# First layer of a channel MLP as seven products of weight and token quarters

## The chip, the core and the metric

The kernel runs on one core of a Trainium2 chip. TensorE (PE) multiplies 128 x 128 weights by up to 512 columns and sums in PSUM; VectorE (DVE), ScalarE (ACT) and GpSimd (POOL) work on tiles in SBUF and PSUM (POOL here on SBUF alone); SyncE (SP) issues the DMAs. PEld is the load of PE's weights beside the running matmul. The metric is the device time in microseconds, lower is better. Before the change the median of 3 runs is 773.5 us (773.27 to 777.58).

## The reference

Three blocks follow each other, all in float32, for 4 batches of 576 tokens and 512 channels (2304 tokens in all):

```python
scores = where(block_i >= block_j, q @ k.T / sqrt(64), -1e9)   # 8 heads of 64, blocks of 64 tokens
x = softmax(scores) @ v
xk, xr = mu_k * x + (1 - mu_k) * x_prev, mu_r * x + (1 - mu_r) * x_prev
k = relu(xk @ w_k)                                             # 512 -> 1024
x = sigmoid(xr @ w_r) * (k * k @ w_v)                          # 1024 -> 512
u = x + (relu(x.T @ w_tok1) @ w_tok2).T                        # 576 -> 256 -> 576, over tokens
out = u + relu(u @ w_ch1) @ w_ch2                              # 512 -> 1536 -> 512
```

## The kernel before

**Precision.** Outside the attention every float32 operand is split into a high part (a cast to PE's fp32r) and a low part (what the cast lost), and a product is three: high x high, high x low, low x high, summed in PSUM. `copy` (L487) makes a high part, `less` (L490) a low one; either may stand on several engines.

**Stages.** The attention comes first. `channel_mix` does the second block, its products in the l banks of PSUM (L961 for the high parts, L966 for the low ones; wx and wy are the two places in SBUF that hold its weights). It stores its result r to DRAM (xd, L1073). `front` does the token MLP of one batch: it loads x from xd (L1094), PE transposes it (L1099), `hidden` (L1123) and `back_in` (L1144) are its two layers, `sum_u` leaves u in the place of x. `back` does the channel MLP in five chunks of the 2304 token columns: chunk 0 has 256, chunks 1 to 4 have 512 each.

**A chunk of the back stage.** ACT and DVE split u (uh, L1245; ul, L1248). Each of twelve groups of 128 hidden channels is 12 matmuls over all columns of the chunk into one of six PSUM banks b (L974); relu takes it to g (L1262, or ACT). The second layer is seven products of quarters already: weights, g and the output are each cut in 2 x 2 quarters, seven sums or differences of g's quarters are multiplied by seven sums or differences of the weight's, and the outputs are added up. `term` (L1204) makes the sums of g, `operand` their high and low parts (op, four buffers), `product` (L1222) is 36 matmuls of 256 columns into one of two PSUM tiles x, with weights that `fetch` (L1213) loads from DRAM wd into one of three buffers rg, 1.5 MB each. `add` (L1295) adds an output to u, the result, which L1300 stores. Chunk 0 does both layers as two plain block products.

**Weights.** The weight of the first layer, c1, lies where channel mix had its own weights (wx), and each half of that is free when channel mix needs it no more (the gates wrfree, wkfree). The weight comes in pieces wst (L516) whose upper 16 bits DVE or ACT bring together (tw, L487), which DVE joins, and of which the high and low parts are written (wx). `load_c2` does the second layer's in twelve column groups: it loads and joins (L1394, L1404), writes the parts into wo, makes the differences of quarters in ws (L1437), writes their parts into wo too and stores wo to wd (L1449).

**Order.** Each step is recorded with its engine or choice of engines; two long tables, RANK (a rank for each step) and ON (its engine), set the order of every engine's queue, and a planner only hands out the buffers. An engine works its queue in order: a step that waits holds up all behind it. Three gates separate stages: sw1 (attention done), sw2 (channel mix done: its PSUM and SBUF become x2, x3, g, the tiles x), sw3 (token MLP and weights done: op1 to op3 and rg).

Of the kernel before, what the change touches and what calls it, by code (L numbers as in the profile page):

```python
# [466 lines left out]
class Kern:  # L467
# [615 lines left out]


    def front(self, b, pool, gate):

        nc, step = self.nc, self.step
        c = {}
        tx = self.tu[b] = Buf()
        self.plan.group = f"f{b}"  # L1090
# [4 lines left out]

# [274 lines left out]
    def load_c2(self, stage):  # L1370
# [5 lines left out]
        for q in range(2 * NH):  # L1376
# [9 lines left out]
            for x in range(2):  # L1386
# [328 lines left out]
```

## Time and profile before

| | us |
|---|---|
| median of 3 runs | 773.5 |
| profiled execution | 776.2 |
| its span | 774.3 |
| PE busy | 754.7 |
| DVE busy | 584.2 |
| ACT busy | 415.7 |
| POOL busy | 276.6 |

The granted TensorE clock is at its upper level in all 40 slices. The span is one execution on the chip by the profiler, and the execution's own time stands above it by what lies around the span. Busy time counts instructions on the engine alone, not its waits. The mean over the span mixes the attention, the token MLP and the back stage, so the slices, the windows and the chain of waits belong to the reading. In a row, "out<-in" are the program's names, and "idle before <-" is the time that the engine stood before such an instruction and what released it. A duration of PE in the groups counts the pipelined instruction whole; the pace of a run of matmuls is its length over their number.

### The profile page before, as it was taken

The page shows a single profiled execution, that of the slowest core. Times are in us where ns is not written, and L with a number is a line of the kernel's source. Part 1 is how long each engine was busy: PE and PEld are TensorE (multiplying, and loading weights), DVE is VectorE, ACT ScalarE, POOL GpSimd, SP SyncE. Part 2 cuts the span into 40 slices and gives each one's busy share as a digit, 9 for nine tenths or more (in the row PEclk, how much of TensorE's full clock was granted, in tenths as well). Part 3 has the DMA queues.
Part 4 walks back from the last instruction along what each step waited for, and adds up shares of the span by engine and source line. Part 5 has one row for each costly group of instructions (what it writes and reads, how often), then busy time and mean ns, then how long its engine had stood idle before and what let it go on. Part 6 is the DMA issues. An engine that isn't in the chain of part 4 may idle for free.

```text
span 774.3 us, 17660 instructions
## 1 busy us (share of the span) xinstructions
PE 754.7 (97%) x6745; PEld 686.5 (89%) x6745; DVE 584.2 (75%) x1336; ACT 415.7 (54%) x1128; POOL 276.6 (36%) x276
## 2 busy tenths in 40 slices
PE   7899999989999999999999999999999999999998
PEld 5677889988999899999999998889989998999997
DVE  8899999988989999895998798744144663974392
ACT  6899988789877787873645455321023112211220
POOL 5441342134433131242434126122343342862351
PEclk9999999999999999999999999999999999999999
DMA  8779894997847867649289857452544644765685
GB/s 273 262 186 215 161 161 114 172 164 134 166 117 127 169 130 153 98 90 291 73 278 292 298 165 244 164 222 93 189 177 163 258 172 175 267 215 215 212 297 202
DMA packets 149700, 146.26 MB, mean 189 GB/s; under 512 B 105456, under 2 KB 127600, under 8 KB 145008
## 3 DMA queue, kind: packets, MB, share of 16 engines
q1 hardware_dynamic: 149616, 145.13, 67.7%
q8 instruction: 53, 0.87, 0.5%
q14 instruction: 31, 0.25, 0.1%
HBM read 98.44 MB, written 22.02 MB: 156 GB/s over the span
## 4 chain that ended last, share of the span: by engine, by line
PE 83%; DMA 8%; DVE 5%; ACT 2%; issue 1%; POOL 0%; SPq 0%; DVEq 0%; ACTq 0%
PE l L961 20%; PE b L974 19%; PE x L1222 16%; PE l L966 9%; DMA pt<-pin 6%; PE s L700 5%; PE o L868 4%; PE b L1123 4%; PE b L1144 3%; PE b L1099 1%; DMA v<-in_v 1%; DVE op L490 1%; DVE nm L737 1%; DMA stage<-in_w_k 1%; ACT pin L494 1%
## 5 line engine op out<-in xcount | busy, mean ns | idle before, releaser
L1222 PEld LDWEIGHTS x<-op,rg 128*128 128x128 f32 x1152 | 141.0, 190 | 3.5 <-DVE x L1295 1.2
L1222 PE MATMUL x<-op,rg 128*128 128x256 f32 x1152 | 141.9, 282 | 1.0 <-DVE x L1295 1.0
L974 PE MATMUL b<-uh,wx 128*128 128x512 f32 (+1 forms) x480 | 142.6, 370 | 0.0
L961 PE MATMUL l<-xh,wx 128*128 128x256 f32 (+1 forms) x768 | 123.3, 301 | 1.4 <-ACT kt L1025 1.4
L961 PEld LDWEIGHTS l<-xh,wx 128*128 128x128 f32 x768 | 107.3, 189 | 8.7 <-issue 2.3
L974 PEld LDWEIGHTS b<-uh,wx 128*128 128x128 f32 x480 | 87.7, 188 | 15.3 <-issue 0.5
L974 PE MATMUL b<-ul,wx 128*128 128x512 f32 (+1 forms) x240 | 88.5, 369 | 0.0
L490 POOL TENSOR_TENSOR op<-g,op 128x512 fp32r<-128x512 f32 x35 | 50.1, 1440 | 106.2 <-DVE op L487 90.6
L961 PE MATMUL l<-kh,wy 128*128 128x256 f32 (+1 forms) x512 | 76.2, 299 | 0.0
L961 PEld LDWEIGHTS l<-kh,wy 128*128 128x128 f32 x512 | 70.3, 189 | 3.0 <-DVE qkl L526 0.8
L783 DVE SCALAR_TENSOR_TENSOR pin<-p,rs,pin 128x384 f16<-128x384 f32 (+3 forms) x104 | 69.0, 676 | 3.8 <-ACT pin L494 3.3
L756 ACT ACTIVATE p<-s,nb 128x384 f32<-128x384 f32 (+4 forms) x120 | 67.0, 562 | 8.5 <-DVE nb L496 3.6
L487 ACT CAST op<-g 128x512 fp32r<-128x512 f32 x33 | 19.9, 620 | 93.5 <-PE x L1222 91.8
L966 PE MATMUL l<-xl,wx 128*128 128x320 f32 (+1 forms) x384 | 66.6, 297 | 0.0
L737 DVE TENSOR_REDUCE nm<-s 128x2 f32<-128x1024 f32 (+4 forms) x80 | 63.9, 801 | 2.9 <-ACT s L729 2.6
L487 DVE CAST op<-g 128x512 fp32r<-128x512 f32 x33 | 21.2, 646 | 49.9 <-PE x L1222 49.8
L490 POOL TENSOR_TENSOR xl<-mt,xh 128x256 fp32r<-128x256 f32 (+1 forms) x40 | 35.3, 889 | 61.8 <-ACT xh L487 48.8
L490 POOL TENSOR_TENSOR kl<-kt,kh 128x256 fp32r<-128x256 f32 (+1 forms) x30 | 27.9, 933 | 81.3 <-ACT kh L487 56.3
L966 PEld LDWEIGHTS l<-xl,wx 128*128 128x128 f32 x384 | 56.2, 189 | 0.4 <-issue 0.2
L868 PEld LDWEIGHTS <-vb 128*64 128x64 f16 x1824 | 45.4, 111 | 11.3 <-issue 8.6
L868 PE MATMUL o<-pt,vb 128*64 128x128 f16 (+1 forms) x1824 | 51.0, 212 | 4.1 <-DMA pt<-pin 4.0
L494 ACT ACTIVATE pin<-p,rs 128x384 f16<-128x384 f32 (+3 forms) x83 | 50.5, 623 | 7.9 <-DMA pt<-pin 5.9
(168 smaller groups left out, 1506.4 us busy)
## 6 DMA issues: line engine op xcount, KB each, us to landing
rg<-wd SPq DMA_DIRECT2D x32, 1536.0 KB, 6.4
wst<-in_w_c SPq DMA_DIRECT2D x48, 256.0 KB, 3.3
wd<-wo SPq DMA_DIRECT2D x12, 1024.0 KB, 5.4
qkf<-in_kq SPq DMA_DIRECT2D x12, 480.0 KB, 4.0
v<-in_v SPq DMA_DIRECT2D x16, 320.0 KB, 3.5
x<-xd SPq DMA_DIRECT2D x4, 1152.0 KB, 8.2
qkl<-in_w_v SPq DMA_DIRECT2D x16, 256.0 KB, 3.7
stage<-in_w_k SPq DMA_DIRECT2D x9, 410.0 KB, 4.1
```

Of the source, the lines that this page charges most:

```text
L487: (self.nc.scalar.copy if e == "A" else self.nc.vector.tensor_copy)(out, x)
L490: (self.nc.vector if e == "V" else self.nc.gpsimd).tensor_tensor(out=out, in0=a, in1=b, op=ALU.subtract)
L494: self.nc.scalar.activation(out=out, in_=x, func=AF.Copy, scale=by)
L700: self.nc.tensor.matmul(o, q[e, q0:q0 + P], k[e, k0:k1], start=n == 0, stop=n == len(terms) - 1)
L737: nc.vector.tensor_reduce(out=c["nm"][:, :nh], in_=m, axis=AX.XY if j == 4 else AX.X, op=ALU.max, negate=True)
L756: nc.scalar.activation(out=c[x], in_=s, func=AF.Exp, scale=0.125, bias=c["nb"][:, x:x + 1], accum_out=c["sm"][:, x:x + 1],)
L783: nc.vector.scalar_tensor_tensor(out=like(pin[:, w:w + n]), in0=c[x], scalar=rs, in1=like(pin[:, :n]), op0=ALU.mult, op1=ALU.subtract)
L868: nc.tensor.matmul(o[hh * D:hh * D + D, q0:q0 + rows], v[:, i, y, hh, :], st["pt", hh, j][:, x * (j + 1) + i, :], start=i == x == y == 0, ...
L961: self.nc.tensor.matmul(ps, ww[:, k, :], x[0][k], start=k == 0 and n == 0, stop=False)
L966: self.nc.tensor.matmul(ps, w[0][:, k, :], x[1][k], start=False, stop=k == kt - 1)
L974: self.nc.tensor.matmul(ps, ww[k], xx[k], start=k == 0 and n == 0, stop=k == kt - 1 and n == 2)
L1222: self.nc.tensor.matmul(ps[:, f * HC:(f + 1) * HC], a[:, k, f, y], t[:, z, k], start=first and n == 1, stop=last and n == 6 * len(ks) * le ...
```

## The change

The first layer of chunks 1 to 4 becomes seven products of quarters as well. u, the weight and g are cut in 2 x 2: u by channel halves (kh) and column halves (t), the weight by hidden halves (fh) and channel halves, g by fh and t. `product1` is three groups of 12 matmuls of 256 columns, one for each pair of hidden groups, into a bank b each. Their sums are made on the u side by `uterm` in two tiles tu, and split by `uoperand` in one of three buffers uo. Outputs are added up in g: `put` copies a bank into g, or adds a bank to what g holds, and after the last addition relu runs over g in place. Three of the four sums of weight quarters are stored to DRAM wc by `load_quads`, `load_c2` made general, and fetched into rg (`sent`) for each chunk; the fourth goes to DRAM ws1 and is put over a quarter of c1 by `swap` when chunk 1 begins. Chunk 0 stays two block products, of 256 columns. RANK and ON are written anew throughout, for 4060 steps where there were 3791. Helpers lie 15 lines further down in the new file (L974 becomes L989, L1222 L1237, L1144 L1159, L1123 L1138, L1099 L1114).

```diff
-    xt0=4, xt1=4, mt=4, xh=8, xl=8, r=4, bxh=2, bxl=2, h1h=2, h1l=2, uh=4, x=2, op=4, rg=3, wo=2, ws=1, ts=2,
+    xt0=4, xt1=4, mt=4, xh=8, xl=8, r=4, bxh=2, bxl=2, h1h=2, h1l=2, uo=3, x=2, op=4, rg=3, wo=2, ws=1, ts=2,
...
 RANK = [int(x) for x in """
-3 15 11 17 0 16 22 13 18 12 6 20 7 4 1 32 24 27 30 34 38 35 43 49 51 56 52 58 69
+21 0 11 5 22 7 10 8 15 6 1 3 13 19 2 37 24 27 30 34 38 35 42 49 51 56 52 58 68 2
...
-        def split(i, b, s, k, o):
...
+        def uoperand(src, cuts):
+            o = Buf("uo")
+            for lo, hi in cuts:
+                w = 2 * (hi - lo)
+
+                def high(e, lo=lo, hi=hi):
+                    self.copy(e, self.uo[o.slot][:, 0, :, lo:hi], src(lo, hi)[0])
+
+                def low(e, lo=lo, hi=hi):
+                    t = self.uo[o.slot]
+                    self.less(e, t[:, 1, :, lo:hi], src(lo, hi)[0], raw(t[:, 0, :, lo:hi]))
+
+                step("any", both(c_a(w), c_v2(w)), high, r=src(lo, hi)[1], w=[(o, (lo, 0))])
+                step("any", both(v=c_v(w), g=c_g(w)), low, r=src(lo, hi)[1] + [(o, (lo, 0))], w=[(o, (lo, 1))])
+            return o
...
+        def uterm(d, a, b, cuts):
+            for lo, hi in cuts:
+                w = 2 * (hi - lo)
+
+                def term(e, lo=lo, hi=hi):
+                    (nc.vector if e == "V" else nc.gpsimd).tensor_tensor(
+                        out=self.tu[d][:, :, lo:hi], in0=a(lo, hi)[0], in1=b(lo, hi)[0], op=ALU.subtract)
+
+                step("any", both(v=c_v(w), g=c_g(w)), term, r=a(lo, hi)[1] + b(lo, hi)[1], w=[(f"tu{d}", lo)])
...
+        def mm1(terms, i, tp):
+            ps, k_ = self.pb[tp.slot], 0
+            for w, o in terms:
+                x = self.uo[o.slot]
+                for k in range(2):
+                    for f in range(2):
+                        for y, z in ((0, 0), (0, 1), (1, 0)):
+                            k_ += 1
+                            nc.tensor.matmul(ps[:, f * HC:(f + 1) * HC], w(2 * i + f, y, k), x[:, z, k],
+                                             start=k_ == 1, stop=k_ == 12 * len(terms))
...
+        def sent(w):
+            r = Buf("rg")
+
+            def fetch():
+                nc.sync.dma_start(raw(self.rg[r.slot]), self.wc[:, w - 1])
+
+            step("S", 0.55, fetch, r=["c1d", "sw3"], w=[r], dma=NH * 4 * P / 704)
+            return (lambda f, y, k: self.rg[r.slot].rearrange("p (f k h m) -> p f k h m", f=NH, k=2, h=2)[:, f, k, y],
+                    lambda i: [r])
+
+        def product1(*terms):
+            tps = [Buf("b") for _ in range(3)]
+            for i in range(3):
+                m = 12 * len(terms)
+                step("PE", c_pe(m * HC, m), mm1, [(w[0], o) for w, o in terms], i, tps[i],
+                     r=[t for w, o in terms for t in w[1](i) + [o]], w=[tps[i]])
+            return tps
+
+        def put(tps, fh, t, plus=None, relu=False):
+            for i in range(3):
+                def put(e, i=i):
+                    out, ps = here(fh, t, i), two_(self.pb[tps[i].slot])
+                    if plus:
+                        nc.vector.tensor_tensor(out=out, in0=ps, in1=here(*plus, i), op=ALU.add)
+                    elif relu and e == "A":
+                        nc.scalar.activation(out=out, in_=ps, func=AF.Relu)
+                    elif relu:
+                        nc.vector.tensor_scalar(out=out, in0=ps, scalar1=0.0, scalar2=None, op0=ALU.max)
+                    else:
+                        self.copy(e, out, ps)
+
+                def relu_(e, i=i):
+                    x = here(fh, t, i)
+                    if e == "A":
+                        nc.scalar.activation(out=x, in_=x, func=AF.Relu)
+                    elif e == "V":
+                        nc.vector.tensor_scalar(out=x, in0=x, scalar1=0.0, scalar2=None, op0=ALU.max)
+                    else:
+                        nc.gpsimd.tensor_scalar(out=x, in0=x, scalar1=0.0, scalar2=0.0, op0=ALU.max, op1=ALU.add)
+
+                step("any", both(None if plus else c_a(NC, True), c_v(NC, True)), put,
+                     r=[tps[i], "sw2"] + (hk(*plus, i) if plus else []), w=hk(fh, t, i))
+                if relu and plus:
+                    step("any", both(c_a(NC), c_v2(NC) + 0.06, c_g(NC)), relu_, r=hk(fh, t, i), w=hk(fh, t, i))
+
+            if c == 1:
+                def swap(y):
+                    d = self.c1k[y][:, 2 * KD:, :].rearrange("p (f a) m -> p f a m", a=KD)[:, :, :2, :]
+                    w = self.ws1[:, y].rearrange("p (f k) m -> p f (k m)", k=2)
+                    nc.sync.dma_start(raw(d).rearrange("p f a m -> p f (a m)"), w)
+
+                for y in range(2):
+                    step("S", 0.6, swap, y, r=["c1d"], w=[("c1", (1, q, y)) for q in range(2 * NH)], dma=2.2)
+            c01, c1_, cut1 = pieces(0, 1), pieces(1), pieces(0)
+            u11 = uoperand(U(0, 0), cut1)
+            uterm(0, U(0, 1), U(0, 0), c01)
+            u21 = uoperand(U(1, 0), cut1)
+            uterm(1, U(1, 1), U(0, 1), c1_)
+            t1 = uoperand(T(0), whole)
+            uterm(0, U(1, 1), T(0), c1_)
+            t2 = uoperand(T(0), whole)
+            uterm(0, U(1, 0), T(0), cut1)
+            t3 = uoperand(T(1), whole)
+            u22 = uoperand(U(1, 1), c1_)
+            t4 = uoperand(T(0), whole)
+            p = product1((block(0, 0), u11))
+            put(p, 0, 0)
+            put(p, 1, 0)
+            put(product1((block(0, 1), u21)), 0, 0, (0, 0), True)
+            put(product1((sent(1), t2)), 1, 0, (1, 0))
+            p5 = product1((block(1, 0), t1))
+            put(p5, 0, 1, (1, 0))
+            put(p5, 1, 1, (1, 0))
+            p = product1((sent(2), t3))
+            put(p, 1, 0, (1, 0))
+            put(p, 1, 1, (1, 1), True)
+            put(product1((sent(3), u22)), 0, 1, (0, 1), True)
+            put(product1((block(1, 1), t4)), 1, 0, (1, 0), True)
...
-    def load_c2(self, stage):
+    def load_quads(self, name, stage, src, store_to, own=None):
         nc, step = self.nc, self.step
-        self.plan.group = "c2"
-        src = self.i["w_c2"].bitcast(U16).rearrange("p a b -> p (a b)")
+        self.plan.group = name
+        src = src.bitcast(U16).rearrange("p a b -> p (a b)")
         n = 2 * P
+        a0 = 4 if own else 0
...
-                o = c["o"].rearrange("p a h b -> p a (h b)")
-                nc.sync.dma_start(self.wd[:, :, q * 2 * P:(q + 1) * 2 * P], raw(o))
+                o = c["o"].rearrange("p a h b -> p a (h b)")[:, a0 + bool(own):]
+                nc.sync.dma_start(store_to[:, :, q * 2 * P:(q + 1) * 2 * P], raw(o))
+                if own:
+                    nc.sync.dma_start(self.ws1[:, :, q], raw(c["o"][:, 4]))
...
-        conv("c1r", lambda: c1r, KD * DM, DM, c1[:, :KD * KD], ["sw1", "wrfree"])
-        conv("c1k", lambda: c1k, NF * DM, DM, c1[:, KD * KD:], ["sw1", "wkfree"])
-        self.load_c2(stage)
+        self.load_quads("c2", stage, self.i["w_c2"], self.wd)
+
+        def own(q, x, y):
+            f, j = divmod(q, 2)
+            return self.c1[NH * x + f][y][:, j:j + 3:2, :]
+
+        self.load_quads("c1", stage, self.i["w_c1"], self.wc, own)
```

SP's queue at the end of channel mix. L1073 stores a part of r; L1094 and L1109 load x of batch 2 (the first) and of batch 3; L516 and L1519 load pieces of weights. Before:

```order
L1073 DMA xd<-r 128x320
L516 DMA wst<-in_w_c 128x1024 x2
L1073 DMA xd<-r 128x320
L516 DMA wst<-in_w_c 128x1024 x3
L1073 DMA xd<-r 128x320
L1094 DMA x_8315<-xd 128x2304
L516 DMA wst<-in_w_c 128x1024 x3
L1094 DMA x_8361<-xd 128x2304
```

Now, where L1580 and L1582 store the weight sums of one column group to wc and ws1:

```order
L1580 DMA wc<-wo 384x1x256
L1582 DMA ws_70<-wo 256x1x128
L1519 DMA wst<-in_w_c 128x1024 x2
L1088 DMA xd<-r 128x320
L1580 DMA wc<-wo 384x1x256
L1582 DMA ws_70<-wo 256x1x128
L1088 DMA xd<-r 128x320
L1109 DMA x_8491<-xd 128x2304
L1519 DMA wst<-in_w_c 128x1024 x2
L1109 DMA x_8539<-xd 128x2304
```

The loads of x still follow the last stores of r; the stores of two column groups have come ahead of them.

PE's queue at the first transposes of batch 2 (x_8315 before, x_8491 now). Between the last product of wy and these transposes stand, before, 48 matmuls of L1144, 24 of L1123 and 12 transposes of batch 1; the last rows of them and what follows:

```order
L1123 MATMUL b_7238<-bxh,w_7252 128x512
L1144 MATMUL b_7236<-w_7253,h1h 128x288
L1144 MATMUL b_7236<-w_7253,h1l 128x288
L1144 MATMUL b_7236<-w_7254,h1h 128x288
L1144 MATMUL b_7236<-w_7253,h1h 128x288
L1144 MATMUL b_7236<-w_7253,h1l 128x288
L1144 MATMUL b_7236<-w_7254,h1h 128x288
L1099 MATMUL b_7239<-ident,x_8315 128x128 x4
L974 MATMUL b_7237<-uh,wx 128x256
```

Now there are 18 of L1159, 16 of L1138 and 4 transposes of batch 1:

```order
L1159 MATMUL b_7212<-w_7229,h1h 128x288
L1138 MATMUL b_7214<-bxh,w_7226 128x512
L1138 MATMUL b_7214<-bxh,w_7227 128x512
L1138 MATMUL b_7213<-bxh,w_7226 128x512
L1138 MATMUL b_7213<-bxh,w_7227 128x512
L1114 MATMUL b_7210<-ident,x_8491 128x128 x4
L1114 MATMUL b_7211<-ident,x_8491 128x128 x4
L1159 MATMUL b_7209<-w_7228,h1h 128x288
```

The transposes of batch 2 have come nearer to the end of channel mix, and no group of the channel layer stands right behind them.

## Rows read from the trace of the kernel before

**Rows 1.** Page, part 1: busy time, share of the span, instructions of each engine.

```profile
PE 754.7 (97%) x6745; PEld 686.5 (89%) x6745; DVE 584.2 (75%) x1336; ACT 415.7 (54%) x1128; POOL 276.6 (36%) x276
```

**Rows 2.** Page, part 2: busy tenths in 40 slices of 19.4 us.

```profile
PE   7899999989999999999999999999999999999998
...
DVE  8899999988989999895998798744144663974392
```

**Rows 3.** Windows: stretch, length, busy us of PE, PEld, DVE, ACT, POOL; clock, DMA.

```profile
360.00:400.00 40.00, 40.00 (x308) 39.13 (x307) 38.51 (x95) 23.10 (x59) 14.79 (x18) 1.00 0.60 202
360.00:500.00 140.00, 139.97 (x964) 130.55 (x963) 124.45 (x299) 74.35 (x176) 50.27 (x63) 1.00 0.70 229
480.00:720.00 240.00, 240.00 (x1496) 216.76 (x1495) 129.24 (x206) 51.19 (x101) 94.68 (x73) 1.00 0.53 192
```

**Rows 4.** Chain of waits, front and back stage: start us, length us, what.

```profile
429.68 1.58 PE b L1144 x12
...
455.05 1.38 PE b L1123 x6
...
511.38 21.79 PE b L974 x96
533.17 8.57 PE x L1222 x72
```

**Rows 5.** Timeline of PE: start us, length us, line, operation, tiles, count.

```profile
428.34 1.34 PE L966 MATMUL l<-kl,wy 128*128 128x320 f32 x8
429.51 0.29 PE L1144 MATMUL b<-w,h1h 128*128 128x288 f32 x1
...
443.04 0.60 PE L1099 MATMUL b<-ident,x 128*128 128x128 f32 x4
```

**Rows 6.** Timeline of SP's queue in the same stretch.

```profile
431.95 0.40 SPq L1073 DMA_DIRECT2D xd<-r  x1
432.44 0.38 SPq L1094 DMA_DIRECT2D x<-xd  x1
```

**Rows 7.** Page, part 6: DMA issues, count, KB each, us to landing.

```profile
rg<-wd SPq DMA_DIRECT2D x32, 1536.0 KB, 6.4
...
x<-xd SPq DMA_DIRECT2D x4, 1152.0 KB, 8.2
```

**Rows 8.** Groups by form: line, engine, operation, tiles, count, busy us, mean ns.

```profile
L490 DVE TENSOR_TENSOR op<-g,op 128x512 fp32r<-128x512 f32 x31 | 27.6, 903 | 0.8 <-ACT op L487 0.8
...
L487 DVE CAST op<-g 128x512 fp32r<-128x512 f32 x33 | 21.2, 646 | 49.9 <-PE x L1222 49.8
...
L1295 DVE TENSOR_TENSOR x<-x,x 128x512 f32<-128x512 f32 x16 | 10.9, 686 | 12.2 <-PE x L1222 10.6 <-POOL x L1295 1.6
...
L487 DVE CAST tw<-wst 128x256 f16<-128x256 bf16 x23 | 9.8, 431 | 1.5 <-DMA wst<-in_w_c 1.1 <-DMA wst<-in_w_t 0.4
...
L490 DVE TENSOR_TENSOR wx<-wst,wx 128x256 fp32r<-128x256 f32 x15 | 6.2, 418 | 0.5 <-ACT wx L487 0.2
...
L490 DVE TENSOR_TENSOR wo<-ws,wo 128x512 fp32r<-128x512 f32 x7 | 5.1, 731 | 0.8 <-ACT wo L487 0.7
...
L1437 DVE TENSOR_TENSOR ws<-wst,ws 128x128 f32<-128x128 f32 x8 | 3.2, 396 | 0.4 <-POOL ws L1437 0.4
...
L490 POOL TENSOR_TENSOR wo<-ws,wo 128x512 fp32r<-128x512 f32 x5 | 7.2, 1440 | 4.4 <-issue 2.8 <-DVE wo L487 1.7
L1437 POOL TENSOR_TENSOR ws<-wst 128x128 f32<-128x128 f32 x12 | 7.2, 600 | 23.0 <-DVE wst L1404 11.0 <-PE l L966 6.2 <-DVE wo L490 2.9
```

**Rows 9.** Groups by line, DVE, all shapes of one line together.

```profile
L1262 DVE TENSOR_SCALAR g<-b 128x512 f32<-128x512 f32 (+1 forms) x27 | 16.8, 635 | 15.4 <-PE b L974 15.3
L1248 DVE TENSOR_TENSOR ul<-x,uh 128x256 fp32r<-128x256 f32 (+7 forms) x32 | 16.0, 548 | 3.9 <-ACT uh L1245 1.9 <-PE b L974 1.9
```

**Rows 10.** Timeline of PE at the end of the run.

```profile
752.92 17.72 PE L1222 MATMUL x<-op,rg 128*128 128x256 f32 x144 [1.02 <-DVE x L1295]
```

**Rows 11.** Tile g: ns min/median/max, first and last start us, tiles.

```profile
L490 DVE TENSOR_TENSOR op<-g,op x31: 674/683/1781, 470.1 to 753.3; 128x512 fp32r<-128x512 f32 x31
```

More of the change, by code (lines that the diff above doesn't have):

```diff
@@ L254 @@
+-----V-----V------V-V---V-V-
 """.split())
@@ L1088, in front @@
         c = {}
-        tx = self.tu[b] = Buf()
+        tx = self.tx_[b] = Buf()
         self.plan.group = f"f{b}"
@@ L1238, in back @@
         self.plan.group = f"b{c}"
-        d = {}
         nt = n // HC
-        def split(i, b, s, k, o):
-            if ("h", i) not in d:
-                d["h", i] = self.bp.tile([P, NC], F32R, tag="uh", name="uh", bufs=BUFS["uh"])
-            nc.scalar.copy(d["h", i][:, o:o + k], self.u[b][:, i, s:s + k])
-        def rest(i, b, s, k, o):
-            nc.vector.tensor_tensor(
-                out=self.ul[:, i, o:o + k], in0=self.u[b][:, i, s:s + k], in1=raw(d["h", i][:, o:o + k]), op=ALU.subtract
-            )
@@ L1252, in g_group @@
-        def g_group(m, tp):
-            ps = d["g", m] = self.pb[tp.slot]
-            x = [d["h", i][:, :n] for i in range(KD)], [self.ul[:, i, :n] for i in range(KD)]
-            self.mm3(ps[:, :n], self.c1[m], x, KD)
-        def g_out(m, e):
-            g = self.g[:, m // NH, m % NH, :n]
-            if e == "A":
-                nc.scalar.activation(out=g, in_=d["g", m][:, :n], func=AF.Relu)
-            else:
-                nc.vector.tensor_scalar(out=g, in0=d["g", m][:, :n], scalar1=0.0, scalar2=None, op0=ALU.max)
@@ L1264, in back, with pieces, u @@
-        tu = [Buf("uh") for _ in range(KD)]
         half = lambda i, s, k: [(i, y) for y in range(2) if s < (y + 1) * HT and s + k > y * HT]
-        x = lambda b, i, s, k: [(self.tu[b], (y, i)) for i, y in half(i, s, k)]
-        for i in range(KD):
+        def pieces(*ts):
+            at = sorted({0, HC} | {o + e - t * HC for t in ts for b, s, k, o in segs for e in (0, k) if 0 < o + e - t * HC < HC})
+            return list(zip(at, at[1:]))
+        def u(kh, t, lo, hi):
             for b, s, k, o in segs:
-                step("A", c_a(k), split, i, b, s, k, o, r=x(b, i, s, k) + ["sw2"], w=[(tu[i], o)])
-                step("V", c_v(k), rest, i, b, s, k, o, r=x(b, i, s, k) + [(tu[i], o), "sw2"], w=[("ul", (i, o))])
@@ L1271, in back @@
-        for m in range(NC1):
-            tp = Buf("b")
-            step("PE", c_pe(12 * n, 12), g_group, m, tp,
-                 r=tu + ["ul"] + (self.need("c1r", m) if m < KD else self.need("c1k", m - KD)), w=[tp])
-            step("any", both(c_a(n, True), c_v(n, True)), g_out, m, r=[tp, "sw2"],
-                 w=[("g", (m // NH, t, m % NH)) for t in range(nt)])
+                if o <= t * HC + lo < o + k:
+                    s0 = s + t * HC + lo - o
+                    toks = [(self.tx_[b], (y, i)) for j in range(2) for i, y in half(2 * kh + j, s0, hi - lo)]
+                    return self.u[b][:, 2 * kh:2 * kh + 2, s0:s0 + hi - lo] if b in self.u else None, toks + [(f"uq{c}", (kh, t)), "sw2"]
@@ new lines, in back @@
+        T = lambda d: lambda lo, hi: (self.tu[d][:, :, lo:hi] if hasattr(self, "tu") else None, [f"tu{d}"])
+        here = lambda fh, t, i: self.g[:, fh, 2 * i:2 * i + 2, t * HC:(t + 1) * HC]
+        hk = lambda fh, t, i: [("g", (fh, t, 2 * i + y)) for y in range(2)]
+        two_ = lambda a: a.rearrange("p (a b) -> p a b", a=2)
+        def mm1(terms, i, tp):
[8 more added lines that the diff above has]
+                                             start=k_ == 1, stop=k_ == 12 * len(terms))
@@ new lines, in block @@
+        def block(fh, kh):
+            return (lambda f, y, k: self.c1[NH * fh + f][y][:, 2 * kh + k, :],
+                    lambda i: [("c1", (fh, 2 * f + k, y)) for f in (2 * i, 2 * i + 1) for k in range(2) for y in range(2)])
+        def sent(w):
[5 more added lines that the diff above has]
+                    lambda i: [r])
@@ new lines, in back @@
+        whole = [(0, HC)]
+        if nt == 1:
+            o1, o2 = [uoperand(U(kh, 0), pieces(0)) for kh in range(2)]
+            for fh in range(2):
+                put(product1((block(fh, 0), o1), (block(fh, 1), o2)), fh, 0, relu=True)
+        else:
+            if c == 1:
[30 more added lines that the diff above has]
+            put(product1((block(1, 1), t4)), 1, 0, (1, 0), True)
@@ L1303, in add @@
                     z = m * len(fs)
-                    step("any", both(v=c_v(z, x.tag == "x"), g=c_g(z) if x.tag != "x" else None), y_out, r=[(x, f) for f in fs], w=toks)
+                    step("any", both(v=c_v(z, x.tag == "x"), g=c_g(z) if x.tag != "x" else None), y_out, r=[(x, f) for f in fs], w=toks + wq)
                     if final:
@@ L1409, in load_c2, with here, high, low @@
                 word = lambda e=e: e["mid"].bitcast(F32).rearrange("p (a b) -> p a b", a=2)
-                def high(en, x=x, word=word, out=out):
-                    self.copy(en, out(0, 2 * x, 2 * x + 2), word())
-                def low(en, x=x, word=word, out=out):
-                    self.less(en, out(1, 2 * x, 2 * x + 2), word(), raw(out(0, 2 * x, 2 * x + 2)))
+                def here(y, x=x, q=q, out=out):
+                    return own(q, x, y) if own else out(y, 2 * x, 2 * x + 2)
+                def high(en, word=word, here=here):
+                    self.copy(en, here(0), word())
+                def low(en, word=word, here=here):
+                    self.less(en, here(1), word(), raw(here(0)))
                 step("S", 0.55, load, r=["sw1"], w=[z], dma=n / 352.0)
@@ L1419, in load_c2 @@
                 step("V", c_v(n), join, r=[z, tt], w=[z])
-                step("any", both(c_a(n), c_v2(n)), high, r=[z], w=[(tw_, (0, x))])
-                step("any", both(v=c_v(n), g=c_g(n)), low, r=[z, (tw_, (0, x))], w=[(tw_, (1, x))])
+                gate, t = [], [(tw_, (y, x)) for y in range(2)]
+                if own:
+                    gate, t = ["wkfree" if x or q // 2 >= KD else "wrfree"], [(name, (x, q, y)) for y in range(2)]
+                step("any", both(c_a(n), c_v2(n)), high, r=[z] + gate, w=t[:1])
+                step("any", both(v=c_v(n), g=c_g(n)), low, r=[z] + t[:1], w=t[1:])
                 mids.append(word)
@@ L1607, in to_second @@
             self.xb = [psx.tile([P, 2 * HC], F32, name=f"x{i}") for i in range(BUFS["x"])]
-            self.ul = self.bp.tile([P, KD, NC], F32R, name="ul")
+            self.uo = [self.bp.tile([P, 2, 2, HC], F32R, name=f"uo{i}") for i in range(BUFS["uo"])]
+            self.tu = [self.bp.tile([P, 2, HC], F32, name=f"tu{i}") for i in range(2)]
             self.g = self.bp.tile([P, 2, NH, NC], F32, name="g")
@@ L1623, in to_back @@
             self.rg = [rg.tile([P, 4 * NH * P], F32R, name=f"rg{i}") for i in range(BUFS["rg"])]
-        convs = [s for s in ready if s.group in ("w_t1", "w_t2", "c1r", "c1k", "c2")]
+        convs = [s for s in ready if s.group in ("w_t1", "w_t2", "c1", "c2")]
         step("X", 0.001, to_back, w=["sw3"], after=fronts + convs)
@@ L1689, in _lay @@
         "w_t2": tiles(inputs["moe2_w_tok2"]),
-        "w_c1": blocks(inputs["moe2_w_ch1"]),
+        "w_c1": eighths(inputs["moe2_w_ch1"]),
         "w_c2": quarters(inputs["moe2_w_ch2"]),
```

86 lines of the change are left out of this document (48 added, 38 removed), and 336 rows, old and new, of the table RANK.

## The prediction

> **What bounds the kernel now.** I read the busy shares first: PE is busy for 97% of the span, DVE for 75% [rows 1]. Averages hide stages, so next the slices: from the tenth of the forty on PE stands at nine tenths or more in each, while DVE holds eight or nine tenths until about the twenty-eighth and then falls, mostly to between three and seven [rows 2]. The windows give the same in numbers: from 480 to 720 us PE is busy for 240.0 of 240 us and DVE for 129.2, POOL for 94.7; from 360 to 500 us, where the weights of both channel layers are converted, DVE is busy for 124.5 of 140 [rows 3]. The chain of waits in the back stage is matmul after matmul with no other engine between [rows 4]. So the back stage is bound by the number and the pace of matmuls, and the stage ahead of it runs DVE nearly full without PE standing still.
>
> **The term that pays.** Rows 4 give the pace: 96 matmuls of 512 columns took 21.79 us, 227.0 ns each; 72 of 256 columns took 8.57 us, 119.0 ns each. Before, chunks 1 to 4 of the first channel layer are 4 x 144 = 576 matmuls of 512 columns: 130.8 us. Afterwards they are 4 x 7 x 36 = 1008 of 256 columns: 120.0 us. Chunk 0 keeps 144 of 256 columns. An eighth of the columns goes, but each column is dearer in short matmuls, so 10.8 us are saved and not 16.4. The Trainium skill (TensorE: Matmul & The Clock Gate, "Back-to-back issue gap") gives a bare gap of N/2.4 + 2.5 ns, which is 215.8 and 109.2 ns here. By that the saving would be an estimated 14.2 us; the trace has both paces 10 ns higher, and I use the trace.
>
> **A wait that the new order makes.** Channel mix ends with a product of wy; its buffers then become the back stage's, and the load of batch 2 (x2) stands behind the last store of r on SP. In the trace that product's first matmul starts at 428.34 us and is done when the next group starts at 429.51 (L1144); the last r is stored at 431.95, x2 is asked for at 432.44, and such a load lands in 8.2 us (median), at about 440.6 [rows 5 to 7]. PE transposes x2 only at 443.04: between lie 48 matmuls of L1144, 24 of L1123 and 12 transposes, 13.5 us of work, so x2 has 2.4 us to spare. In the new order (the PE fence of the change) there are 18 of L1144's kind, 16 of L1123's and 4 transposes: 18 x 0.132 + 16 x 0.230 + 0.60 = 6.7 us, 0.132 and 0.230 us being the paces of rows 4 (12 in 1.58 us, 6 in 1.38 us) and 0.60 us what four such transposes take [rows 5]. x2 lands 440.6 - 429.5 = 11.1 us after the mix, so PE stands for 11.1 - 6.7 = 4.4 us. The new stores of weight sums stand ahead of it on SP too; each waits for its last low part and could make it later. I take 4.4, with 0 as the lower end (if PE comes late) and 9 as the upper (a store held up by one conversion round, some 4 us).
>
> **Conversion of w_c1.** Each of its twelve column groups now gets four differences, one rounding of 512 words and one low part. By the order DVE has 23 more differences (0.40 us), nine more 512-word low parts (0.73), and gives up nine casts of tw (0.43) and six smaller instructions (0.42 at most): 9.2 + 6.6 - 3.9 - 2.5 = 9.4 us more [rows 8]. POOL gets 25 differences at 0.60, three low parts at 1.44 and two smaller ones: some 21 us more. ACT gets some 14 us more and has 65 idle in 360 to 500 us. DVE has 15.5 us idle there [rows 3], so its 9.4 fit, but only just, and channel mix of the last batch shares DVE with it. Bounds for PE: 0 us (in 360 to 400 us DVE was busy for 38.5 of 40 and PE for all 40 [rows 3]) and 15 us (what POOL gets and DVE's idle time cannot cover). I take 2, near the lower end, because rows 3 show PE undisturbed at 96% of DVE.
>
> **Sums in place in the back stage.** DVE gets 96 additions from PSUM into g. The nearest row is the addition of x from PSUM, 0.686 us: 65.9 us. It also gets 13 copies from PSUM (at the same 0.686: 8.9), 19 relus in place (as the cast of op, 0.646: 12.3), operands of u (10 casts, 13 low parts and 10 differences, all of 512 words, at 0.65 to 0.9: about 25, against 16.0 for the ul parts that go), and 11 low parts of op (0.903) less 8 casts (4.7); 27 evictions go (16.8) [rows 8, 9]. Net about +84 us. With the 129 of rows 3 that is 213 us in the 229 that PE then needs: 93%. PE waits nowhere at 96% in 360 to 400 us, so the lower end is 0; the upper end is the third rival's. I take 1.
>
> **Edits with no price.** Twelve more fetches of 1.5 MB and 6.3 MB of stores: a fetch lands in 6.4 us [rows 7] and the DMA engines are 0.53 busy from 480 to 720 us [rows 3]; ten fetches a chunk instead of seven would make that about 0.75. The cover is that a fetch starts three buffers ahead; without it each would cost its 6.4 us. The filler matmuls of the start go from 193 to 186, which is nothing. The last seven products of the second layer, 252 matmuls, close both orders; in the trace the last four of them ran on end behind a gap of 1.0 us [rows 10].
>
> **The sum.** The profiled execution took 776.2 us (span 774.3), 2.7 above the median of 773.5. 776.2 - 10.8 + 4.4 + 2 + 1 = 772.8, and 2.7 less on the scale of the median: **770**.
>
> **Rivals.**
> (1) *The forecast*: most of the saving is given back ahead of the back stage: 766 to 778. Chance 0.47.
> (2) *The whole saving arrives.* PE reaches the transposes of x2 late, because something ahead held it, and the wait is hidden; DVE keeps up. 773.5 - 10.8 = 762.7, with a microsecond or two of waits 761 to 765. For it: PE was undisturbed at every load of DVE that the trace shows. Against it: 6.7 us of work cannot cover 11.1. Chance 0.31.
> (3) *DVE and POOL block each other until DVE is the bound: slower.* A low part of op on DVE took 0.674 us at the least and 1.781 at the most [rows 11], 0.903 in the mean: the long ones lie under a POOL instruction. After the change POOL has about 34 us more in the back stage (16 low parts and eight relus at 1.44, 15 differences near 1.0, less 11 low parts of op), 129 of 229 us, and DVE some 165 instructions that work from SBUF to SBUF. If each of them that meets POOL waits for half a POOL instruction (129/229 = 0.56; 0.56 x 0.72 us x 165 = 67 us, of which about 33 is in the means already), DVE needs 213 + 34 = 247 us and PE stands for 18; the conversion stage, with POOL's 21 us, would add 5 to 10. 773.5 - 10.8 + 4.4 + 18 + 5 = 790; this decides once all stalls together pass 18.5 us. Against it: the additions from PSUM, the largest new load, showed 0.686 us in the mean of all sixteen, near the evictions from PSUM (0.635 with the shorter ones) [rows 8, 9]. The Trainium skill (SBUF — State Buffer, "Who interferes with whom") says the same as a rule: GpSimd and DVE lock a shared port pair for a whole instruction when DVE has two SBUF inputs or copies SBUF to SBUF in its fast mode, and never when DVE has at most one SBUF input otherwise. By that rule the additions are clean and the rest is not; the trace agrees in both. Chance 0.17.
> (4) The order of the attention stage, searched anew, moves the time by itself, either way, by more than 8 us; nothing in the rows speaks for it. Chance 0.05.
>
> **How the numbers follow.** About 1%, 7.7 us, is what a measurement of this kernel can tell from no change. Below 765.8 lies case 2 and half of case 4: 0.33. Above 781.2 lie case 3, part of its milder form counted in case 1, and the rest of case 4: 0.20. Within 1%: 0.47. The range takes in cases 1 and 2 with the milder half of case 3: 760 to 784.
>
> **What would show it.** Right: matmuls into b of 256 columns at 119 ns; a PE gap of 3 to 6 us ahead of the first transposes of x2, ended by the load of x; PE without gaps from there to the last product; additions into g near 0.69 us; DVE near 90% in the back stage. Wrong: no gap at x2 (case 2); PE gaps in the back stage ended by DVE or POOL writing op, uo or g (case 3); fetches of rg that end PE's gaps; a start of the back stage that has moved by more than 5 us for another reason.

## The result: slower, not faster

The changed kernel took 778.7 us (median of 8 runs, 775.4 to 780.2), the kernel before 773.7 in the same measurement: 1.0059 of it, 95% interval 1.0032 to 1.0086. Three further measurements beside the kernel before gave 1.0104 (1.0079 to 1.0129), 1.0070 (1.0043 to 1.0097) and 1.0078 (1.0049 to 1.0106). The forecast was 770, a gain of 0.4%.

The first traced executions mislead: that of before lay 2.5 us above its median, that of the changed kernel 3.3 below. I therefore read a second execution of each. Page, part 1, of the changed kernel's second execution (782.9 us), answering [rows 1]:

```profile
span 781.1 us, 18822 instructions
...
PE 748.4 (96%) x7170; PEld 700.1 (90%) x7170; DVE 672.7 (86%) x1454; ACT 435.6 (56%) x1165; POOL 336.7 (43%) x334
```

The same lines of the kernel before's second execution (775.0 us):

```profile
span 773.3 us, 17660 instructions
...
PE 754.6 (98%) x6745; PEld 685.5 (89%) x6745; DVE 584.5 (76%) x1336; ACT 415.7 (54%) x1128; POOL 276.1 (36%) x276
```

The windows of both by stage tell where PE stood (columns as in [rows 3]): up to 340 us, to the end of channel mix, to the last L1144 (L1159), to the end. The changed kernel first:

```profile
0.00:340.00 340.00, 322.91 (x3774) 287.65 (x3776) 306.74 (x795) 284.60 (x849) 114.90 (x132) 1.00 0.75 163
340.00:447.00 107.00, 100.97 (x817) 95.58 (x816) 87.73 (x215) 59.93 (x148) 41.54 (x52) 0.98 0.83 265
447.00:518.50 71.50, 68.38 (x449) 62.18 (x448) 55.16 (x116) 33.17 (x68) 41.21 (x51) 0.95 0.66 213
518.50:781.10 262.60, 256.17 (x2138) 254.69 (x2137) 223.03 (x329) 57.93 (x100) 139.07 (x99) 1.00 0.77 283
```

The kernel before:

```profile
0.00:340.00 340.00, 327.34 (x3845) 291.55 (x3846) 310.00 (x815) 286.31 (x849) 113.17 (x127) 1.00 0.77 163
340.00:427.20 87.20, 86.82 (x701) 84.43 (x701) 71.52 (x170) 42.74 (x105) 30.28 (x38) 1.00 0.75 228
427.20:510.30 83.10, 82.18 (x523) 72.96 (x522) 62.44 (x149) 38.83 (x88) 23.40 (x31) 1.00 0.59 190
510.30:773.30 263.00, 258.27 (x1683) 236.60 (x1681) 140.56 (x203) 47.80 (x88) 109.29 (x80) 1.00 0.58 210
```

Length less PE's busy time is PE's idle time: 17.1, 6.0, 3.1 and 6.4 us in the changed kernel, 12.7, 0.4, 0.9 and 4.7 before. That is 14.0 us more, spread over every stage. PE's work itself shrank as forecast: an execution of the changed kernel in which the granted clock stayed at its upper level (a third one, span 771.8) has PE busy for 743.5 us, 11.1 under 754.6:

```profile
PE 743.5 (96%) x7170; PEld 696.2 (90%) x7170; DVE 671.1 (87%) x1454; ACT 436.3 (57%) x1165; POOL 335.9 (44%) x334
```

But in the second execution it is 748.4, and the clock column shows why: 0.98 and 0.95 in the two middle stages. So 781.1 - 773.3 = 7.8 = -11.1 (less work) + 4.9 (work at the lower clock) + 14.0 (stops). The third execution shows the other end: no lower clock and 28.3 us of stops, 9.6 more than before, so 771.8 - 773.3 = -1.5 = -11.1 + 9.6.

What PE waited for in the changed kernel (list of waits: total us, times, longest):

```profile
PE o L883 <- DMA pt<-pin: 7.1, 6, 2.2
PE l L976 <- ACT kt L1040: 4.1, 3, 2.5
...
PE b L1114 <- DMA x<-xd: 3.0, 1, 3.0
PE x L1237 <- DVE x L1419: 2.1, 2, 1.3
```

The third line is the wait that the prediction named. PE's timeline around it:

```profile
452.23 0.43 PE L1159 MATMUL b<-w,h1h 128*128 128x288 f32 x2
452.49 0.29 PE L1159 MATMUL b<-w,h1l 128*128 128x288 f32 x1
...
453.02 1.78 PE L1138 MATMUL b<-bxh,w 128*128 128x512 f32 x4
457.81 1.97 PE L1114 MATMUL b<-ident,x 128*128 128x128 f32 x8 [3.02 <-DMA x<-xd]
459.43 0.59 PE L1159 MATMUL b<-w,h1h 128*128 128x288 f32 x1
459.82 0.44 PE L1159 MATMUL b<-w,h1l 128*128 128x288 f32 x1
```

A matmul of 288 columns takes 0.29 us ahead of the stop and 0.44 to 0.59 behind it: the granted clock is at its lower level, 1.2 instead of 2.4 GHz. The windows of 5 us there:

```profile
455.00:460.00 5.00, 2.19 (x10) 2.19 (x11) 4.56 (x9) 3.30 (x7) 4.29 (x6) 0.70 1.00 346
460.00:465.00 5.00, 5.00 (x25) 4.89 (x24) 3.12 (x9) 1.95 (x5) 3.29 (x6) 0.62 1.06 373
465.00:470.00 5.00, 5.00 (x37) 4.83 (x37) 4.05 (x10) 2.99 (x7) 1.31 (x4) 1.00 0.56 176
```

The same windows show DMA engines that are full (shares of 1.00 and 1.06). That matters below.

### The profile page after: what moved, and what is told of

Read it like the earlier page. It is cut to its first block, busy times and chain, and to the rows that moved or that the text cites. A ratio compares the mean times of both kernels' runs of the same rounds, so it can differ in the third digit from the quotient of the medians.

```text
span 773.6 us, 18822 instructions
## 1 busy us (share of the span) xinstructions
PE 743.7 (96%) x7170; PEld 697.2 (90%) x7170; DVE 672.1 (87%) x1454; ACT 436.1 (56%) x1165; POOL 336.2 (43%) x334
## 4 chain that ended last, share of the span: by engine, by line
PE 58%; DVE 17%; DMA 13%; ACT 7%; issue 2%; POOL 2%; SPq 1%; DVEq 0%; ACTq 0%; POOLq 0%
PE l L976 14%; PE b L1308 12%; PE x L1237 10%; PE l L981 7%; DMA pt<-pin 6%; PE s L715 5%; PE o L883 4%; PE b L1159 3%; DMA wst<-in_w_c 2%; DVE op L505 2%; DVE g L1338 2%; PE b L1138 2%; DVE op L502 2%; ACT p L771 1%; DVE g L1219 1%
## 5 line engine op out<-in xcount | busy, mean ns | idle before, releaser
L1237 PE MATMUL x<-op,rg 128*128 128x256 f32 x1152 | 143.6, 282 | 3.1 <-DVE x L1419 2.7
L1237 PEld LDWEIGHTS x<-op,rg 128*128 128x128 f32 x1152 | 139.8, 190 | 4.1 <-DVE x L1419 3.3
L1308 PE MATMUL b<-uo,wx 128*128 128x256 f32 x720 | 92.3, 282 | 0.0
L1308 PEld LDWEIGHTS b<-uo,wx 128*128 128x128 f32 x720 | 88.8, 190 | 0.5 <-DVE x L1166 0.2
L1338 DVE TENSOR_TENSOR g<-b,g 128x512 f32<-128x512 f32 x96 | 63.4, 684 | 11.2 <-PE b L1308 10.3
L505 POOL TENSOR_TENSOR kl<-kt,kh 128x320 fp32r<-128x320 f32 (+1 forms) x33 | 30.5, 925 | 94.0 <-ACT kh L502 48.5
L798 DVE SCALAR_TENSOR_TENSOR pin<-p,rs,pin 128x512 f16<-128x512 f32 (+3 forms) x104 | 66.2, 646 | 3.7 <-ACT pin L509 3.1
L502 ACT CAST op<-g 128x512 fp32r<-128x512 f32 x40 | 24.4, 620 | 54.4 <-DVE g L1351 11.9
L505 POOL TENSOR_TENSOR op<-g,op 128x512 fp32r<-128x512 f32 x29 | 43.3, 1498 | 26.0 <-ACT op L502 14.3
L1308 PE MATMUL b<-uo,rg 128*128 128x256 f32 x432 | 54.2, 281 | 0.0
L1308 PEld LDWEIGHTS b<-uo,rg 128*128 128x128 f32 x432 | 52.5, 189 | 0.0
```

Of the source, the lines that this page charges most:

```text
L502: (self.nc.scalar.copy if e == "A" else self.nc.vector.tensor_copy)(out, x)
L505: (self.nc.vector if e == "V" else self.nc.gpsimd).tensor_tensor(out=out, in0=a, in1=b, op=ALU.subtract)
L798: nc.vector.scalar_tensor_tensor(out=like(pin[:, w:w + n]), in0=c[x], scalar=rs, in1=like(pin[:, :n]), op0=ALU.mult, op1=ALU.subtract)
L1237: self.nc.tensor.matmul(ps[:, f * HC:(f + 1) * HC], a[:, k, f, y], t[:, z, k], start=first and n == 1, stop=last and n == 6 * len(ks) * le ...
L1308: nc.tensor.matmul(ps[:, f * HC:(f + 1) * HC], w(2 * i + f, y, k), x[:, z, k], start=k_ == 1, stop=k_ == 12 * len(terms))
L1338: nc.vector.tensor_tensor(out=out, in0=ps, in1=here(*plus, i), op=ALU.add)
```

## Experiments

Ratios are to the kernel before, measured beside it on the same chip; a difference between variants is one of ratios, 0.1% being 0.8 us. The intervals of two ratios together leave such a difference uncertain by 2.4 to 3 us: differences of 3.4 us and more are clear of zero, those of 1 to 2 us are not. "Lost clock" is one less a run's mean granted clock, times its span, averaged over the runs. RANK and ON do not fix the order alone: the planner hands out the steps that are ready by its own costs and landing times, the lowest rank first, so a variant that changes an engine or a landing time also moves other steps. "Theory D" below is that a stop of PE of some 2 us or more is followed by some us at the lower granted clock; the third execution of the changed kernel, read for it, has a stop of 2.69 us at x2 and no lower clock behind it, so it holds for most stops and not for every one.

**Second executions.** No edit.

> The changed kernel, unaltered, for a second execution in the trace. The first one took 775.4 us, 3.3 below the median of its runs, with PE busy 743.7 us and idle 6.0 us from 350 to 500 us, 2.4 in the back stage. Theory A (the DMA engines are full while w_c1 is converted and channel mix ends): an execution near the median, 778 to 779 us, has its further 3 us of PE idle time between 350 and 500 us. Theory B (DVE and POOL block each other in the back stage): the further 3 us lie behind 510 us. Theory C (the attention's new order): they lie ahead of 350 us, at matmuls that wait for transposing DMAs. PE's busy time stays at 743.7 within 1 us by all three.

> The kernel before, unaltered, for a second execution in the trace; the first took 776.2 us, 2.5 above the median. By all theories PE is busy for 754.7 us within 1 us and has no gap from 350 to 750 us. If the execution takes 772 to 774 us, what is missing against the first is idle time of PE ahead of 350 us by theory C, and busy time nowhere.

1.0104; the ledger above is from these two. Of the further 7.5 us of span 2.8 are stops, and they lie where theory A puts them: 8.9 us of stops from 350 to 500 us, 6.0 in the first trace (counting those of 0.3 us or more). The larger part, 4.7 us of PE's busy time above the first trace's, no theory had expected. The kernel before took 775.0 us, not 772 to 774, and stands for 1.1 us from 350 to 500 us, not for none.

**DMA.** Leave out the stores of sums; then also seven eighths of the stores of wd.

```diff
-                if own:
-                    nc.sync.dma_start(self.ws1[:, :, q], raw(c["o"][:, 4]))
...
-                nc.sync.dma_start(store_to[:, :, q * 2 * P:(q + 1) * 2 * P], raw(o))
+                if not own:
+                    nc.sync.dma_start(store_to[:, :1, q * 2 * P:(q + 1) * 2 * P], raw(o[:, :1]))
```

> The changed kernel without the 24 stores of weight sums (6.3 MB) to wc and ws1; the fetches of sums and the swap read wd in their place, as many bytes, so the products of sums are of wrong weights. All conversions stay and the order of every engine too. Theory A: the weight pieces land earlier, channel mix ends earlier, x2 with it: 3 to 5 us faster than the changed kernel, 774 to 776 us, and DMA share below 0.9 from 400 to 450 us where it was 1.0. Theories B and C: within 1 us of the changed kernel, 778 to 779.

> The changed kernel without the stores of weight sums to wc and ws1 and with an eighth of the stores of wd (17 MB fewer in all); all fetches read the eighth that is written, as many bytes each, so the products of both layers are of wrong weights. Order and conversions stay. Theory A (full DMA engines delay weight pieces, and with them ACT, whose queue then holds up channel mix): the stops of PE from 380 to 470 us fall from 6 to 9 us to under 3, the clock stays at 1.0 there, 7 to 10 us faster than the changed kernel. Rival (the pieces are late because SP and the buffers of pieces hold them up, not the DMA engines): 4 to 5 us faster, as without the sums' stores alone, with the stops of 384 to 430 us still there.

Without the sums' stores: 1.0055 (1.0034 to 1.0076) beside 1.0104, 3.8 us. The stop at x2 falls to 0.55 us, and lost clock from 3.9 to 1.6 us:

```profile
453.67 1.09 PE L1114 MATMUL b<-ident,x 128*128 128x128 f32 x8 [0.55 <-DMA x<-xd]
```

The stops behind kt (1.4 and 0.95 us at 401 and 429) stay; in the changed kernel the first store of sums is issued behind such stops, at 437.6 us in the first trace and 443.6 in the second. With few stores: 1.0003 (0.9982 to 1.0023) beside 1.0070, 5 us; expected were 7 to 10, and the rival had 4 to 5. This variant also lacks stores that the kernel before has. The windows from 400 to 450 us, of the changed kernel's first execution:

```profile
400.00:450.00 50.00, 47.59 (x305) 44.38 (x303) 44.11 (x108) 30.55 (x71) 24.01 (x31) 1.00 1.01 338
```

The kernel before (first execution):

```profile
400.00:450.00 50.00, 49.98 (x324) 46.26 (x323) 42.58 (x102) 26.95 (x63) 15.96 (x19) 1.00 0.83 275
```

With few stores:

```profile
400.00:450.00 50.00, 49.47 (x315) 45.82 (x315) 47.28 (x112) 31.35 (x73) 26.34 (x34) 1.00 0.61 189
```

The DMA share went from 0.83 to 1.01, and PE lost 2.4 us; with the share at 0.61 PE loses 0.5. The stop at x2 is down to 0.2 us there, the clock stays up (lost clock 0.7 us, 3.4 in the changed kernel), and behind kt there is one of 0.38 us left at 424. The three at 384 to 394 us remain (1.5, 0.5, 0.5): they wait for DVE and ACT, not for a transfer. So both gains are about what the stop at x2 and the clock make up: 2.5 + 2.3 us without the sums' stores, 2.5 + 2.7 with few stores. Ahead of x2 the stores matter little: from 340 us to the load of x2 PE is idle for 3.0 to 6.0 us in the four traces of the changed kernel, 4.7 without the sums' stores, 3.1 with few stores, and 0.1 and 0.4 before.

**Attention.** The order and engines of the kernel before for 2373 early steps (RANK and ON only).

> The changed kernel with the order and the engines of the kernel before for 2373 steps of the attention and its channel mix, up to about 335 us; the rest as changed. Theory C (the new order of the attention costs what PE idles there: 15.7 and 16.8 us ahead of 350 us against 14.2 and 12.2 before): 2 to 4 us faster than the changed kernel. Theory A or D alone (the loss is made from 380 to 470 us): within 1 us of it.

1.0026 (1.0004 to 1.0048) beside 1.0070: 3.4 us, as theory C has it. PE's idle time up to 340 us is 13.5 us in its trace (14.8 to 18.6 in the four traces of the changed kernel, 12.7 and 14.8 before), and its waits for pt<-pin there are 3.4 us (4.8 to 7.4, and 4.0 in both).

**The wait for x2.** First, later transposes; second, matmuls to fill the wait; third, a load in pieces.

```diff
-        add("S", 0.475, load, r=gate + [f"xd{b}"], w=[tx], dma=3.28)
+        add("S", 0.475, load, r=gate + [f"xd{b}"], w=[tx], dma=3.28 + 6.5 * (b == 2))
...
+        for n, key in ((3163, 3052.1), (3164, 3052.11), ..., (3156, 3052.6)):
+            self.plan.steps[n].key = key
```

```diff
+            if b == 2 and i == 2:
+                for _ in range(16):
+                    nc.tensor.matmul(ps, self.w1[0][:, 0, :P], self.w2[0][:, 0, :512], start=True, stop=True)
```

```diff
-            nc.sync.dma_start(c["x"], self.xd[b])
+            cuts = ((2 * P, 3 * P), (0, 2 * P), (3 * P, S)) if b == 2 else ((0, S),)
+            for lo, hi in cuts:
+                nc.sync.dma_start(c["x"][:, :, lo:hi], self.xd[b][:, :, lo:hi])
```

> The changed kernel with the first three transposes of x2 (and the first two hidden products behind them) put behind seven groups of the second token layer of batch 1 in PE's order. By the wait that the prediction named (3.1 us in the trace of the changed kernel): that gap falls to under 1 us and the time by 1.5 to 3 us, 776 to 777 us. A rival: the chain of batch 2 (transpose, split, hidden layer) then comes late itself and PE waits there for as long: no change, 778 to 779 us.

> The changed kernel with 16 more matmuls of 512 columns (3.6 us at 227 ns) in PE's queue right ahead of the first transposes of x2, into the bank that these overwrite, from weights that lie there long before: PE works while it waits for x2. Theory D: the wait stays, the granted clock behind it stays at 1.0, and the 2 to 3 us that the lower clock cost there are saved: 1.5 to 3 us faster than the changed kernel. Rival (the idle time itself is the whole cost): no change, or up to 1 us slower where the matmuls outlast the wait.

> The changed kernel with the load of x2 in three pieces of 128, 256 and 192 token columns, the piece that PE transposes first ahead. By theory D with the wait that the prediction named: the stop of 2.7 to 3.1 us at these transposes falls to under 1 us, and the lower clock behind it goes with it (2 to 3 us in most executions): 3 to 5 us faster than the changed kernel, mean clock 0.998 or more. Rival (the DMA engines are full there, so the first piece lands no earlier than half of the whole): 0 to 2 us faster.

Later transposes (the planner is also told that x2 lands 6.5 us later): 1.0132 beside 1.0104, no gain; the rival was right, PE now stands at h1h, h1l, bxh and wx instead (0.7, 1.4, 0.6 and 0.5 us). Filled: 1.0059 beside 1.0070, no gain that can be told from none, where 1.5 to 3 us were expected; but lost clock falls from 3.4 to 1.4 us, and the trace has 1.0 in all windows there. In that trace x2 lands at 455.9 us and the filling matmuls end only at 456.5, so they outlast the wait and give back part of what the clock gives. In pieces: 1.0056 beside 1.0078, 1.7 us, not clear of zero; lost clock 1.1 instead of 3.0; two stops of 0.65 and 1.00 us are left, so between the two expectations.

**A stop made in the kernel before.** Load x2 twice there.

```diff
-            nc.sync.dma_start(c["x"], self.xd[b])
+            for _ in range(2 if b == 2 else 1):
+                nc.sync.dma_start(c["x"], self.xd[b])
```

> The kernel before with x2 loaded twice, the second load waiting for the first, so that PE has to stop ahead of its transposes there too: 8.2 us of a load less the 2.4 it had to spare, some 5 to 6 us. Theory D (a stop of PE lowers the granted clock behind it, in whichever kernel): mean clock 0.993 to 0.997 where the kernel before has 0.9996 to 1.000, and the time rises by the stop and 2 to 4 us more: 780 to 785 us. Rival (the lower clock belongs to the changed kernel's denser work): mean clock stays at 0.999 or more, and the time rises by the stop alone, 779 to 781.

1.0072 (1.0044 to 1.0099), 780.1 us; lost clock 3.9 us instead of 0.3. PE's timeline in it:

```profile
444.38 0.63 PE L1100 MATMUL b<-ident,x 128*128 128x128 f32 x4 [1.96 <-DMA x<-xd]
446.51 0.55 PE L974 MATMUL b<-uh,wx 128*128 128x256 f32 x1 [1.49 <-DVE x L1152]
```

And its windows:

```profile
445.00:450.00 5.00, 3.51 (x14) 2.92 (x13) 4.07 (x11) 3.15 (x8) 1.49 (x2) 0.50 1.00 389
450.00:455.00 5.00, 5.00 (x17) 3.66 (x17) 4.04 (x9) 3.72 (x10) 0.86 (x2) 0.50 0.49 152
```

The stops together are shorter than I expected (3.5 us; the second load landed in 5.1 us, not in 8.2), but behind them the clock is at 0.50 for two windows. So the lower clock comes with the stops in the kernel before too, and needs no changed work.

**The back stage.** Give ACT the 47 casts of op and uo that DVE did (ON: V becomes A).

> The changed kernel with the 47 casts of op and uo that DVE did moved to ACT, order by the same ranks. The mild form of theory B (PE's stops of 2.1 to 2.7 us in the back stage, at products that wait for DVE's additions into x, come from a DVE that is held up, its casts at 1.5 us under POOL instead of 0.43): the stops fall to under 1 us and the time by 1 to 2 us. Rival (the stops are the order's: the addition stands behind other work whatever its length): within 1 us of the changed kernel.

1.0026 (1.0007 to 1.0045) beside 1.0078: 4 us, more than expected. Stops of 0.3 us or more from 500 to 750 us fall from 2.2 to 0.9 us; behind 510 us the order of DVE, ACT and POOL has moved too, so it is casts and order together. Ahead of 510 us all queues are the same as in the changed kernel, so what the edit gives must lie behind it. There, from the last L1159 to the last matmul, the trace takes 258.1 us, the four traces of the changed kernel 258.6, 258.7, 259.0 and 260.1. So the traces show 0.5 to 2.0 us; the rest of the 4 is ahead of the first difference, the same program's change from run to run.

**All together**, and with the planner's landing times set later.

> The changed kernel with the attention's order of the kernel before, x2 loaded in three pieces, and the casts on ACT. If the three shares add up (2.5 for the attention, 3 to 5 for x2 and the clock, 1 to 2 for the casts): 6.5 to 9.5 us faster than the changed kernel, 0.997 to 1.000 of the kernel before. If they overlap: 1.002 to 1.005.

> The combined kernel with the planner told that pieces of the token and channel weights land 1 us later, so that conversions stand later in the queues of ACT and DVE, behind channel mix's evictions. Theory A in its queue form (ACT stands at a cast of a piece that has not landed, with channel mix's kt behind it): the stops of PE at kt, 1 to 2.5 us near 400 and 428 us, fall to under 0.5 and the time by 1 to 3 us against the combined kernel: 0.994 to 0.997 of the kernel before. Rival (later conversions make chunk 0 wait for its weights): slower than the combined kernel by up to 8 us.

```diff
+        for s in self.plan.steps:
+            if s.eng == "S" and s.group in ("w_t1", "w_t2", "c1", "c2"):
+                s.land += 1.0
```

Combined: 0.9975 (0.9954 to 0.9996), and 0.9987 (0.9971 to 1.0003) in a second measurement: 772.7 us beside 774.9, 772.8 beside 774.1. The three together take the whole loss back, 8 us beside the changed kernel, clear of zero. The shares nearly add up (0.44 + 0.22 + 0.52 = 1.2% against 1.0078 - 0.9975 = 1.0%), each by itself with the uncertainty told above. It is the fastest version, ahead of the kernel before by some 0.2%, hardly more than is measurable. Later landing: 1.0070, the rival's outcome. The stops behind kt near 400 and 428 us are gone (one of 1.3 us stands at 388), but chunk 0 then waits for its weights (2.1 us on ACT's wx, 1.1 on POOL's), and lost clock is 6.6 us.

## Why the prediction was wrong

Three terms that stood at nothing were not nothing: the clock behind a stop, the stores of sums, the attention's order; a fourth, the conversion, was too small. By the two second executions stops grew by 4.4 us up to 340 us (nothing forecast), 5.6 to the end of channel mix (2 forecast), 2.2 to the last L1159 (4.4 forecast) and 1.7 behind it (1 forecast), and the lower clock added 4.9 (nothing forecast).

**The term that pays** was right: 10.8 us forecast, 11.1 measured.

**The wait for x2** was right in its place and its releaser, and near in its size (4.4 forecast, 2.6 to 3.1 us in four traces), in part by luck: it was worked out for the new order with the stores at nothing, and without the stores of sums the stop is 0.55 us. x2 then lands 7.6 us after the mix, with them 9.9 to 10.5, where 11.1 were forecast. What failed is that a stop was priced at its length. Behind it the clock column (windows of 5 us, one less the clock, times the length) shows 0, 1.7, 3.4 and 3.4 us more in the four traces; over whole runs lost clock is 2.3 to 3.9 us in the four measurements of the changed kernel, 0.1 to 0.3 in the kernel before. The row was there to read, though the slices hide it: a 9 there is any clock of 0.9 or more, so 40 nines are not the upper level throughout. A window of the first trace of before, around a stop of 2.0 us at 26.4 us, in an execution 2.5 us above the median:

```profile
25.00:30.00 5.00, 3.59 (x24) 2.81 (x25) 4.99 (x18) 4.89 (x20) 2.37 (x3) 0.73 0.69 216
```

The Trainium skill (TensorE: Matmul & The Clock Gate, "HAM oscillation — how this bites in real kernels") says that a wait for a transfer between groups of matmuls brings the clock down and that the next group starts at half of it. Most traces agree (0.70 and 0.62 behind 3.0 us, 0.50 behind 2.0 and 1.5), one does not (1.00 behind 2.69 us).

**"Edits with no price"** failed beside it. It priced 6.3 MB of stores at nothing by the DMA share of 480 to 720 us (0.53), while they run from 437 to 499 us, right behind the twelve stores of wd, which the new order has drawn together: in the first traces they go from 366 to 434 us, where before there was a pause from 420 to 463, around the load of x2. The share was 0.83 from 400 to 450 us already and became 1.01. That is paid at x2: in the four traces it is asked for 0.7 to 1.5 us after the last part of r is made and lands in 6.9 to 7.3 us; without the stores of sums these are 0.5 and 5.7 us, the stop all but goes, and the kernel gains 3.8 us.

**The conversion** was mis-sized: 2 us forecast, 3.0 to 6.0 of idle time from 340 us to the load of x2. Its 2 us were read from DVE's idle time; what PE waits for there is kt of ACT (1.1 to 4.1 us) and bxl and r of DVE (1.4 to 1.8 us together). ACT works its queue in order, and kt stands behind the cast of a weight piece that has not landed. ACT's timeline in the second execution of the changed kernel:

```profile
400.96 0.48 ACT L502 CAST tw<-wst 128x256 f16<-128x256 bf16 x1 [3.56 <-DMA wst<-in_w_t]
401.31 0.41 ACT L502 CAST wo<-wst 128x256 fp32r<-128x256 f32 x1
401.62 0.44 ACT L1040 ACTIVATE kt<-l 128x320 f32<-128x320 f32 x1
```

PE's first matmul behind this kt stood for 2.5 us. This piece landed in 6.2 us; in the other three traces it took 3.6 to 3.8, and no stop of 2.5 us is there. How far the stores make such pieces late is not shown: PE is idle there for 4.7 us without the sums' stores and for 3.1 with few stores. Why the new order stops there at all stays open.

**The attention's order** was given 0.05 and no price; it costs 3.4 us.

**Sums in place** were near: 1 us forecast, 2.1 to 2.4 measured (stops from 500 to 750 us). The additions took 0.682 us (0.686 forecast), DVE was busy for 193 of 229 us (213 forecast), the DMA share is 0.74 (0.75 forecast), and PE's idle time is behind additions into x. Group and window of the execution with the clock at its upper level:

```profile
L1338 DVE TENSOR_TENSOR g<-b,g 128x512 f32<-128x512 f32 x96 | 63.4, 682 | 11.7 <-PE b L1308 10.9
```

```profile
490.00:719.00 229.00, 226.36 (x1876) 224.44 (x1875) 193.41 (x295) 53.28 (x93) 123.06 (x90) 1.00 0.74 271
```

So the third rival, a DVE that becomes the bound, did not happen; its cause is seen in the cast of op (0.42 us in the median, 1.52 at the most, and all ten long ones of 26 lie under a POOL instruction), and relief of DVE took stops away. What came true is the first case past its own bounds: the saving was given back ahead of the back stage, by many small stops (12.2 of the 14.0 us of further stops lie there, more than the 11.1 saved) and by the clock behind them, which no case had.

## What to carry to other kernels

Read the share of DMA and the idle time of a resource in the very stretch where the added work runs. Price a stop of PE at its length and the slower matmuls behind it; where the clock column dips in one execution of before, that row gives a first price. Take the scale from several executions: two traces from opposite ends of their spread hid 6 us here.

## What was unexpected

Stops of 1.96 and 1.49 us with 0.6 us of transposes between them left a clock of 0.50 in two windows of 5 us; single stops of 1.0 to 1.3 us in the back stage left it at 1.00. A stop of 2.69 us in one trace (span 771.8) left it at 1.00 too, and one of 3.02 us in another did not, so the same program differs by this from run to run. Cutting a stop in two need not save the clock either: in the second execution of the combined kernel, with x2 in pieces, two stops of 1.03 and 1.45 us stand at 449.6 and 451.8 us, and the clock in the windows there is 0.58 and 0.74:

```profile
450.00:455.00 5.00, 3.55 (x18) 3.30 (x17) 4.56 (x8) 3.55 (x7) 3.84 (x4) 0.58 1.04 372
455.00:460.00 5.00, 5.00 (x28) 4.88 (x28) 3.11 (x8) 1.64 (x5) 3.31 (x5) 0.74 1.05 375
```
